# Four attention layers: the full layers start on their first twelve key tiles before the last keys exist

## The chip, the cores and the metric

The kernel runs on one core of one Trainium2 chip, in one launch. The metric is the device time of that launch in microseconds. Engines are named as the profile does: PE (TensorE matmul), PEld (its weight loads), DVE (VectorE), ACT (ScalarE), POOL (GpSimd) and SP (SyncE, whose queue issues the DMAs).

## The reference

Four layers of attention on 2048 tokens of width 512, 32 heads of 16. Layers 0 and 2 see a window of 256 keys, layers 1 and 3 ("full layers") all 2048.

```python
qkv = (x @ wqkv).reshape(B, S, 3, H, Dh).transpose(2, 0, 3, 1, 4)
scores = einsum("bhqd,bhkd->bhqk", q, k) * Dh ** -0.5      # window layers: masked to 0 <= i - j < 256
o = einsum("bhqk,bhkd->bhqd", softmax(scores), v)
x = x + o.transpose(0, 2, 1, 3).reshape(B, S, D) @ wo      # once per layer, on layernorm(x)
```

## The kernel before

**Tiles.** The tokens form four chunks of 512 (NQ), the heads eight quads of 4 (NQD) or four head groups of 8 (NHT). A full layer visits query chunks and quads (layer 1: chunk by chunk, all eight quads; layer 3: head group by head group, four chunks of two quads each). One visit (attn_full, line 805) walks 16 key tiles of 128 keys (NT). Each tile takes two score groups on PE (line 764), two exponentials on ACT (line 772) and, two score groups later, one P V group on PE (line 817), which sums into the pair of accumulators acc. After the 16th tile the epilogue (line 719) joins the two accumulators and normalises.

**The shift.** The exponential needs a bound on the scores. It comes from the largest squared key length of each head group: the key projection (keys, line 566) is followed by a product that sums squares (squares, line 548), a maximum on DVE (line 575), and, after the last chunk, key_shift (line 609), which writes the shift into row 7 of the keys in DRAM (kf). Only then may the keys of that head group be loaded into tiles kt (load_full, line 781).

**Side work.** Projections of other chunks and layers are Work objects: K1 and K3 (keys of the last chunk of layer 1, and of layer 3, by head group), Q, Q3 (queries), VV (values; half 0 are the first 16 heads), OO and O3 (output projection), T (transposes of the normalised rows by DMA). A Side (line 943) issues some of their matrix products after each tile. In a full layer each product is cut in 8 small matmuls, all products share one pair of PSUM banks (PH["halves"], lines 380 and 386), and each group of twelve is read out by two DVE steps (join, line 425) before the next may begin. Side.finish (line 1010) forces what is left of a list.

**The order.** The program writes PE's and DVE's instructions in the order in which they shall run in the full layers, by a clock that it keeps itself (clock, vt_). Between a window layer and the following full layer stands the tail (line 1231): the values of layer l + 1, the last output projection OO(l, 3) with the normalisation of the last chunk, its transposes, K1(0) and K1(1) or K3(3, 0), and two tiles of the last values (lasts, line 1233). The full layer starts when that is done. Its first keys and queries are loaded early (early_keys, early_queries, lines 629 to 637), and the shift of head group 0 is written into the loaded tile directly (line 622).

In layer 1 the list works[1][0] is spread over the first 64 tiles (quads 0 to 3 of chunk 0), works[1][1] over the rest. The keys of quads 2, 4 and 6 need the shifts of head groups 1, 2 and 3; a loop asks for them one quad ahead: 

```python
while (l, c, qd % 2) == (1, 0, 1) and qd + 1 in qds and ("S", 1, (qd + 1) // 2) not in DONE:
```

The generator wo (OO) ends its fourth step with the normalisation, in one of two places:

```python
            if i == 3 and not PH["full"]:
                if not tail:
                    yield "freed", clock[0]
                yield from norm(l + 1, c, xs, tail)
            yield last(MM)
        if PH["full"]:
            yield from norm(l + 1, c, xs, tail)
```

Of the kernel before, what the change touches and what calls it, by code (L numbers as in the profile page):

```python
# [19 lines left out]
P = 128  # L20
NT = S // P
# [169 lines left out]
def fast_path(ctx, tc, flag, a_x, a_wqkv, a_wo, b_wqkv, b_wo, out):  # L191
# [20 lines left out]
    XC, XN, V, O, OT, KM, PH = {}, {}, {}, {}, {}, {}, {"free": 0.0, "busy": False}  # L212
# [353 lines left out]
    def keys(l, c, act, ht=None, then=None, ring=0):  # L566
# [11 lines left out]
        pend.append((clock[0] + (4.6 if PH["full"] else 3.6 if PH["win"] else 1.2), rest))  # L578

    def queries(l, c, act, ht=None, ring=0):  # L580
# [23 lines left out]
        pend.append((clock[0] + (4.6 if PH["full"] else 3.6 if PH["win"] else 1.2), rest))  # L604
# [5 lines left out]
    def key_shift(l, ht):  # L610

        r = quarters(ht)
        kx = vp.tile([P, 1], F32, name=f"kx{l}_{ht}", tag="kx")
        nc.vector.tensor_reduce(kx[r], KM[l][r], axis=AX.X, op=ALU.max)
# [4 lines left out]
        nc.vector.tensor_scalar(m[r], ones[r], kx[r], -0.515, op0=ALU.mult, op1=ALU.mult)  # L619
        if ht == 0:  # L620
            for pr in range(2):
                nc.sync.dma_start(PRE["k"][7:P:R, pr, :].rearrange("r (c n) -> r c n", n=QC),
                                  m[2 * pr:2 * pr + 2, None, :].broadcast_to([2, 2, QC]))
        nc.sync.dma_start(rows(kf)[8 * ht:8 * ht + 8, 7, :].rearrange("h (c n) -> h c n", n=QC),
                          m[32 * ht:32 * ht + 8, None, :].broadcast_to([8, NQ, QC]))
        DONE["S", l, ht] = clock[0]

    PRE = {}

    def early_keys(l):  # L630

        PRE["k"] = pp.tile([P, 2, S // 2], F16, name=f"kt{l}_0_0_0", tag="kt", bufs=3)
        nc.sync.dma_start(PRE["k"], kf[0:2, :, :S // 2].rearrange("r p n -> p r n"))

    def early_queries(l):

        PRE["q"] = pp.tile([P, 2, QC], F16, name=f"qt{l}_0_0", tag="qt", bufs=3)
        nc.sync.dma_start(PRE["q"], qs[1, 0][0:2].rearrange("r p n -> p r n"))

# [78 lines left out]
    def epilogue(l, c, qd, a):  # L718
# [7 lines left out]
        with tc.high_priority(HEAD_START if l % 2 else 0):  # L726
            if l % 2:
                a = vp.tile([P, QC], F32, name=f"sa{n}", tag="j")
                join(a, acc, 1.0)
                vec(0.7)  # L730
# [21 lines left out]
        if u:  # L752
            soon(1, 1.2, parts)

# [26 lines left out]
    def load_full(l, c, qd):  # L781
        n = f"{l}_{c}_{qd}"
        pair = slice(2 * qd, 2 * qd + 2)
        qt, kts = PRE.pop("q", None), [PRE.pop("k")] if "k" in PRE else []
        if qt is None:
            qt = pp.tile([P, 2, QC], F16, name=f"qt{n}", tag="qt", bufs=3)
            nc.sync.dma_start(qt, qs[1, c][pair].rearrange("r p n -> p r n"))
        for v in range(len(kts), 2):
            kt = pp.tile([P, 2, S // 2], F16, name=f"kt{n}_{v}", tag="kt", bufs=3)
            nc.sync.dma_start(kt, kf[pair, :, v * S // 2:(v + 1) * S // 2].rearrange("r p n -> p r n"))  # L790
            kts.append(kt)
        return kts, qt

# [11 lines left out]
    def attn_full(l, c, qd, kt, qt, a):  # L805
        for j in range(NT):
# [6 lines left out]
            def pv(j=j, es_=es_):  # L813
                for h in range(4):
                    for r in range(2):
                        k = slice(R * r, R * r + R)
                        nc.tensor.matmul(acc[r][32 * h:32 * h + DH + 1, :], V[l, qd // 4, j // 8][k, j % 8, 4 * (qd % 4) + h, :],  # L817
                                         es_[h // 2][k, h % 2, :], start=(j == 0), stop=(j == NT - 1),
# [103 lines left out]
    class Side:  # L922
# [65 lines left out]
        def share(self):  # L988

            self.budget = min(self.budget + max((self.cost - self.spent) / max(self.steps - 3 - self.k, 1), self.least), 0.75)  # L990
            self.lag = max(self.lag - 0.42, -0.3)
# [5 lines left out]
            while (self.q and clock[0] >= PH["free"] and self.budget >= MM / 2 and (self.lag < 0.25 or self.budget > 0.45)  # L997
                   and self.spent - s0 < 1.5 * MM):
# [26 lines left out]
    def attention(l, works):  # L1025
# [3 lines left out]
        load = load_win if win else load_full  # L1029
        sd = None  # L1030
        for t in range(NHT if l == 3 else 1):
            for c in range(NQ):
                qds = range(2 * t, 2 * t + 2) if l == 3 else range(NQD)
                if l == 1:

                    sd = sd or Side(NT * NQD // 2, works[0], works[1], 0.33)
                    while ("Q", 1, c) not in DONE or pend and PH["busy"]:
                        sd.one(True)
                    settle()
                else:  # L1040
                    sd = Side((3 if win else NT) * len(qds), works[t * NQ + c], works[t * NQ + c + 1], 0.34 if l == 3 and t < 2 else 0.0)
                ahead = deque([PRE.pop("w", None) or load(l, c, qds[0])])
                if win:
                    ahead.append(load(l, c, 1))
                for qd in qds:
                    if (l, c, qd) == (1, 0, NQD // 2):
                        sd.finish()
                        sd = Side(NT * NQD * NQ - NT * NQD // 2, works[1], works[2], 0.33)
                    while (l, c, qd % 2) == (1, 0, 1) and qd + 1 in qds and ("S", 1, (qd + 1) // 2) not in DONE:
                        if ("K1", (qd + 1) // 2) in DONE and not PH["busy"]:  # L1050
                            settle()
                        else:
                            sd.one(True)
# [243 lines left out]
```

## Time and profile before

| | us |
|---|---|
| median of 3 runs | 2691.59 (2689.32 to 2695.28) |
| the profiled execution | 2692.26 |
| its span, first to last instruction | 2690.2 |
| PE busy, ACT busy, DVE busy | 2474.9, 2363.6, 1107.5 |
| mean granted clock of PE | 0.991 |

All times in the profile count from the start of the span. Matmuls are pipelined and their ends are modelled, so PE's cost is better read from the distance between starts than from busy time. The row of a group gives start, duration, engine, line, operation, tiles and shapes, and in brackets the idle time before it with what ended it.

### The profile page before, as it was taken

How to read it: one execution, taken by the hardware profiler on the slowest of the kernel's cores; microseconds unless marked ns; L12 is line 12 of the kernel's file. 1: busy time of each engine (PE TensorE's matmuls, PEld its weight loads, DVE VectorE, ACT ScalarE, POOL GpSimd, SP SyncE). 2: the span in 40 equal slices, each digit the busy share in tenths (PEclk: the TensorE clock that was granted, in tenths of full speed). 3: DMA queues.
4: the chain of work that ended last, by engine and by line, in shares of the span. 5: the costliest groups of instructions: out<-in, count | busy, mean ns of one | idle time of the engine just before them, and what ended most of it. 6: DMA issues, size and time to landing. Idle time of an engine off the chain costs nothing.

```text
span 2690.2 us, 120844 instructions
## 1 busy us (share of the span) xinstructions
PE 2474.9 (92%) x54767; PEld 1133.5 (42%) x54767; DVE 1107.5 (41%) x2350; ACT 2363.6 (88%) x2671; POOL 531.8 (20%) x1072
## 2 busy tenths in 40 slices
PE   7889999999998999999999999899999999999997
PEld 3344444444443444444444444544444443433332
DVE  5576453223334434434236666232333323333333
ACT  4666764999999999999996776699999999999997
POOL 1556550000000100100116886010000000000000
PEclk9999999999999999999999999999999999999999
DMA  8889875232334325324227666433333323334332
GB/s 281 254 274 268 236 198 155 69 97 86 110 94 120 97 91 148 103 87 115 92 77 211 189 171 166 128 95 105 98 97 97 106 77 114 106 98 126 126 118 93
DMA packets 341189, 361.29 MB, mean 134 GB/s; under 512 B 117800, under 2 KB 256568, under 8 KB 334392
## 3 DMA queue, kind: packets, MB, share of 16 engines
q1 hardware_dynamic: 340664, 353.46, 44.2%
q8 instruction: 430, 7.05, 1.1%
q14 instruction: 95, 0.78, 0.1%
HBM read 240.65 MB, written 96.99 MB: 126 GB/s over the span
## 4 chain that ended last, share of the span: by engine, by line
ACT 55%; PE 23%; issue 11%; DVE 6%; DMA 3%; SPq 1%; POOL 0%; ACTq 0%; DVEq 0%; POOLq 0%
ACT e L772 55%; PE b L406 7%; PE acc L850 4%; PE acc L817 3%; PE s L764 2%; PE s L768 2%; PE bs L409 2%; PE b L409 2%; PE b L402 1%; DMA kt<-kw 1%; DVE xh L461 1%; DVE xn L455 0%; DMA qs<-sp 0%; SPq L483 0%; DVE xh L455 0%
## 5 line engine op out<-in xcount | busy, mean ns | idle before, releaser
L772 ACT ACTIVATE e<-s 128x1024 f32<-128x1024 f32 (+2 forms) x2432 | 2241.6, 1056 | 143.2 <-PE s L768 104.5
L817 PE MATMUL acc<-e,vt 64*17 64x512 f32 x16384 | 1094.6, 590 | 1.9 <-issue 1.9
L764 PE MATMUL s<-qt,kt 64*32 64x512 f16 x16384 | 860.0, 381 | 123.9 <-ACT e L772 97.1
L764 PEld LDWEIGHTS <-kt 64*32 64x32 f16 x16384 | 408.2, 89 | 935.1 <-issue 853.8
L817 PEld LDWEIGHTS acc<-e,vt 64*17 64x17 f32 x16384 | 283.8, 92 | 67.9 <-issue 8.1
L843 POOL TENSOR_SCALAR_AFFINE_SELECT e<-e 128x256 f32<-128x256 f32 x512 | 230.5, 457 | 154.8 <-ACT e L772 154.1
L840 POOL TENSOR_SCALAR_AFFINE_SELECT e<-e 128x256 f32<-128x256 f32 x448 | 201.5, 456 | 96.5 <-ACT e L772 93.2
L850 PE MATMUL acc<-e,vt 128*17 128x384 f32 (+2 forms) x2816 | 202.6, 390 | 2.5 <-POOL e L840 2.2
L749 POOL TENSOR_TENSOR oh<-o,oh 128x512 f16<-128x512 f32 x31 | 36.1, 1165 | 725.1 <-DVE oh L748 725.1
L428 DVE TENSOR_SCALAR sa<-acc 128x512 f32<-128x512 f32 x64 | 44.3, 691 | 291.3 <-PE acc L817 291.3
L406 PE MATMUL b<-xc,w 128*32 128x512 f16 x2496 | 152.4, 389 | 10.8 <-DVE km L575 6.9
L714 DVE SCALAR_TENSOR_TENSOR x<-b,x 128x512 f32<-128x512 f32 x122 | 84.0, 689 | 175.1 <-PE b L402 168.4
L534 POOL TENSOR_TENSOR sq_h<-sp_h 128x512 bf16<-128x512 f16 x29 | 43.0, 1483 | 562.4 <-DVE sp_h L528 562.4
L768 PE MATMUL s<-qt,kt 64*128 64x384 f16 (+2 forms) x1408 | 120.8, 276 | 28.2 <-ACT e L772 22.7
L534 POOL TENSOR_TENSOR sq<-sp 128x512 bf16<-128x512 f16 x32 | 45.8, 1434 | 496.8 <-DVE sp L528 473.6
L402 PE MATMUL b<-xc,w 64*32 64x512 f16 x3072 | 126.4, 376 | 1.5 <-DVE j L429 0.8
L428 DVE TENSOR_SCALAR vt<-b 128x256 f32<-128x256 f32 (+1 forms) x36 | 18.4, 512 | 233.8 <-PE b L402 219.9
L402 PE MATMUL b<-wo,oh 64*32 64x512 f16 x2592 | 109.1, 376 | 4.1 <-DVE m_None L591 1.8
L402 PE MATMUL b<-xc,w_h 64*32 64x512 f16 x2784 | 111.8, 376 | 0.1
L428 DVE TENSOR_SCALAR j_h<-b 128x512 f32<-128x512 f32 x29 | 20.1, 692 | 214.6 <-PE b L402 214.6
L406 PEld LDWEIGHTS <-w 128*32 128x32 f16 x2496 | 73.5, 99 | 79.2 <-issue 27.7
L768 PEld LDWEIGHTS <-kt 64*128 64x128 f16 x1408 | 52.2, 94 | 125.7 <-issue 105.3
(142 smaller groups left out, 1942.3 us busy)
## 6 DMA issues: line engine op xcount, KB each, us to landing
kt<-kf SPq DMA_DIRECT2D x128, 512.0 KB
qt<-qs SPq DMA_DIRECT2D x128, 256.0 KB
xd<-x SPq DMA_DIRECT2D x96, 256.0 KB
x<-xd SPq DMA_DIRECT2D x96, 256.0 KB
w<-wd SPq DMA_DIRECT2D x21, 1024.0 KB
kt<-kw SPq DMA_DIRECT2D x64, 256.0 KB
qs<-sp SPq DMA_DIRECT2D x48, 256.0 KB
wo<-wd SPq DMA_DIRECT2D x12, 1024.0 KB
```

The costliest lines, as they stand in the source:

```text
L402: nc.tensor.matmul(ps[g:g + 32, r], a[k, g:g + 32], b[k], start=(i == 0), stop=(i == len(pairs) - 1), skip_group_check=True)
L406: nc.tensor.matmul(ps[g:g + 32], a[:, g:g + 32], b, start=(i == 0), stop=(i == len(pairs) - 1), skip_group_check=True)
L409: nc.tensor.matmul(ps, a, b, start=(i == 0), stop=(i == len(pairs) - 1))
L534: nc.gpsimd.tensor_tensor(sq, sp[:, 0], sp[:, 0], ALU.mult)
L714: nc.vector.scalar_tensor_tensor(xs[i], p, 1 / WS, xs[i], op0=ALU.mult, op1=ALU.add)
L764: nc.tensor.matmul(ps[g:g + 32, h], kt[R * h:R * h + R, pr, kc + g:kc + g + 32], qt[R * h:R * h + R, pr], start=True, stop=True, skip_grou ...
L768: nc.tensor.matmul(ps[:, h, s0:s0 + wd_], kt[R * h:R * h + R, pr, kc:kc + P], qt[R * h:R * h + R, pr, qc:qc + wd_], start=True, stop=True)
L772: nc.scalar.activation(e[:, :, w0:w1], ps[:, :, w0:w1], AF.Exp, scale=SCALE)
L817: nc.tensor.matmul(acc[r][32 * h:32 * h + DH + 1, :], V[l, qd // 4, j // 8][k, j % 8, 4 * (qd % 4) + h, :], es_[h // 2][k, h % 2, :], star ...
L840: nc.gpsimd.affine_select(v, v, pattern=[[0, 2], [-1, P]], compare_op=ALU.is_gt, fill=0.0, base=0, channel_multiplier=1)
L843: nc.gpsimd.affine_select(v, v, pattern=[[0, 2], [1, P]], compare_op=ALU.is_ge, fill=0.0, base=0, channel_multiplier=-1)
L850: nc.tensor.matmul(a[32 * h:32 * h + DH + 1, q * P:(q + nb) * P], V[l, (4 * c + j) // 4][:, j % 4, 4 * qd + h, :], es_[h // 2][:, h % 2, s ...
```

## The change

The full layers begin while the keys of the last chunk (512 keys, the last four tiles) do not exist yet.

- key_shift takes a number of chunks. first_loads calls it with three as soon as the window layer is done, and loads the queries, the first eight and the next four key tiles of quads 0 and 1.
- The visits of chunk 0, quads 0 and 1, are split: part A has tiles 0 to 11 of each, part B tiles 12 to 15 of each. After part A the sums are kept (park). When K1(0) or K3(3, 0) is done, key_shift writes the final shift, computes the ratio of the two exponentials into SH, and load_last fetches the last four tiles. The epilogue of part B multiplies the parked sums by the ratio and adds the new ones.
- Work leaves the tail for the side lists: T, K1(0) or K3(3, 0), the values of the last chunk; in layer 1 also K1(1) and the second half of values 1, in layer 3 also values of chunk 2. K1(3) goes from the first list of layer 1 to the second. OO(l, 3) is now of the kind without tail, and what is left of the tail when all its works are done or "freed" is carried into the full layer.
- In parts A and B ("rush") a tile may take 2.5 products of side work instead of 1.5, with a budget of 0.75 us.
- Keys of the next visit are loaded during a visit if they are complete, and otherwise when the visit begins, after its key projection and shift have been forced.

The core of the diff:

```diff
+    def first_loads(l):
+        key_shift(l, 0, NQ - 1)
+        HELD[0], HELD[1] = load_full(l, 0, 0), load_full(l, 0, 1)
+        load_more(l, 0, 0, HELD[0][0], True)
...
+    def park(l, c, qd):
+        drain(2)
+        a = PARK[c, qd] = vp.tile([P, QC], F32, name=f"pk{l}_{qd}", tag=("wa", "wc")[qd], bufs=1)
+        with tc.high_priority(HEAD_START):
+            join(a, acc, 1.0)
...
+    def load_last(l):
+        for qd in range(2):
+            nc.sync.dma_start(HELD[qd][0][1][:, :, S // 4:], kf[2 * qd:2 * qd + 2, :, 3 * S // 4:].rearrange("r p n -> p r n"))
...
+                if (c, qd) in PARK:
+                    nc.vector.scalar_tensor_tensor(a, PARK.pop((c, qd)), SH[l][:, 2 + qd:3 + qd], acc[0], op0=ALU.mult, op1=ALU.add)
+                    nc.vector.scalar_tensor_tensor(a, acc[1], 1.0, a, op0=ALU.mult, op1=ALU.add)
...
+        if not win:
+            visits[:2] = [(0, 0, qd, js) for js in (range(NT - 4), range(NT - 4, NT)) for qd in range(2)]
...
+            if (l, c, qd) == (1, 0, NQD // 2):
+                sd.finish()
+                sd = Side(NT * NQD * NQ - NT * NQD // 2, works[1], works[2], 0.33)
+            if not win and not part_a and (rest is None if part_b else not ahead):
+                while lacking(c, qd) or owing(c, qd):
+                    if lacking(c, qd) or PH["busy"]:
+                        sd.one(True)
+                    else:
+                        settle()
...
+                while part_a and u == 6 and ("V", l, 2, (0,), 0) not in DONE:
+                    sd.one(True)
+                while part_b and qd == 0 and u in (1, 3) and ("V", l, 3, (0,), u - 1) not in DONE:
+                    sd.one(True)
...
-    works = [[side0(c) for c in range(NQ)], [[last_lower(1), K1(2), upper(1, 2), upper(1, 3), K1(3)], side1()], [side2(c) for c in range(NQ)],
+    works = [[side0(c) for c in range(NQ)], [[T(1, 3), K1(0, True), VV(1, 3, False, (0,), (), range(2)), last_lower(1), K1(1, True), VV(1, 1, False, (1,)), K1(2, True), upper(1, 2), upper(1, 3)], side1()], [side2(c) for c in range(NQ)],
...
-    tails = {0: [VV(1, 2, True, (0,)), OO(0, 3, True), VV(1, 1, True, (0, 1), late(1)), VV(1, 0, True, (1,), late(1)), T(1, 3), K1(0, True), K1(1, True)],
-             2: [VV(3, 0, True, (0,)), OO(2, 3, True), VV(3, 1, True, (0,), late(3)), VV(3, 2, True, (0,), late(3)), VV(3, 0, True, (1,), late(3)), T(3, 3), K3(3, 0, True, True)]}
+    tails = {0: [VV(1, 1, True, (0,)), VV(1, 2, True, (0,)), OO(0, 3), VV(1, 0, True, (1,))],
+             2: [VV(3, 0, True, (0,)), VV(3, 1, True, (0,)), OO(2, 3)]}
```

What this does to the order of the instructions, at three places. First ACT where layer 1 begins (sp_1_3_h and sq_1_3_h are the products and squares of K1, vt the values, e the exponentials). Before:

```order
L519 ACTIVATE sp_1_3_h_0_7995<-bs_7982 128x512
L532 ACTIVATE sq_1_3_h_0_7998<-sp_1_3_h_0_7995 128x512
L519 ACTIVATE sp_1_3_h_1_8025<-b_8002 128x512
L532 ACTIVATE sq_1_3_h_1_8028<-sp_1_3_h_1_8025 128x512
L670 ACTIVATE vt_0_1_7684<-b_8034 128x16x16
L670 ACTIVATE vt_0_1_7684<-b_8056 128x16x16
L772 ACTIVATE e_0_0_0_0_8094<-s_0_0_0_0_8085 128x1024
```

And now:

```order
L672 ACTIVATE vt_1_0_7922<-bs_7924 128x16x16
L672 ACTIVATE vt_1_0_7922<-b_7938 128x16x16
L672 ACTIVATE vt_1_0_7922<-bs_7952 128x16x16
L672 ACTIVATE vt_1_0_7922<-b_7966 128x16x16
L786 ACTIVATE e_0_0_0_0_7996<-s_0_0_0_0_7987 128x1024
```

K1(0), K1(1) and the values of the last chunk no longer stand ahead of the first exponential.

Second, PE between quads 3 and 4 of layer 1, chunk 0 (s_0_3_15_1 is the last score group of quad 3, s_0_4_0_0 the first of quad 4). Before, 48 matmuls of K1(3) stand between them:

```order
L764 MATMUL s_0_3_15_1_11188<-qt_0_3_9609,kt_0_3_1_9613 32x512
L402 LDWEIGHTS w_1_3_h_10103
L402 MATMUL b_8076<-xc_3_7836,w_1_3_h_10103 32x512
...
L764 LDWEIGHTS kt_0_4_0_10433
L764 MATMUL s_0_4_0_0_11256<-qt_0_4_10431,kt_0_4_0_10433 32x512
```

Now there are 288 matmuls of the values of chunk 2, 384 of the values of chunk 3, together seven groups of 96 with a join after each, and the squares of K1(2):

```order
L778 MATMUL s_0_3_15_1_11183<-qt_0_3_9643,kt_0_3_1_10086 32x512
...
L402 MATMUL b_7986<-wv_2_1_0_9400,xc_2_7065 32x256
...
L402 MATMUL b_7986<-wv_3_1_0_10702,xc_3_8069 32x256
...
L556 MATMUL b_7986<-sq_1_3_h_2_10940,hsum 32x512
...
L778 MATMUL s_0_4_0_0_11894<-qt_0_4_11888,kt_0_4_0_11890 32x512
```

The same place on SP (mk_2 is the shift of head group 2, kt_0_4_0 the first keys of quad 4, kt_0_3 those of quad 3, w and wv weights). Before:

```order
L624 DMA kf<-mk_2_9250 8x4x512
L790 DMA kt_0_3_0_9611<-kf 128x2x1024
L787 DMA qt_0_4_10431<-qs_0_101 128x2x512
L373 DMA w_1_3_h_10103<-wd_1_110 128x8x128
L790 DMA kt_0_3_1_9613<-kf 128x2x1024
L790 DMA kt_0_4_0_10433<-kf 128x2x1024
```

And now:

```order
L798 DMA qt_0_6_12844<-qs_0_101 128x2x512
L371 DMA w_0_1_11954<-wd_0_109 128x4096
L371 DMA w_0_2_11956<-wd_0_109 128x4096
L620 DMA kf<-mk_2_11885 8x4x512
L808 DMA kt_0_4_0_11890<-kf 128x2x1024
```

The shift of quad 4 was stored before the keys of quad 3 were loaded; now it is stored right before quad 4's own keys.

Third, DVE early in layer 3, where the normalisation of chunk 3 ends (xn, xh its parts, mv the statistics, v, y, z the scaling). Before:

```order
L455 TENSOR_SCALAR xn_3_3_36886<-x_15_36718,mv_3_36796,y_3_36851 128x512
L461 TENSOR_TENSOR xh_3_3_36887<-xn_3_3_36886,xh_3_3_36887 128x512
L522 SCALAR_TENSOR_TENSOR sp_1_3_h_0_37085<-b_37072,sp_1_3_h_0_37085 128x512
L575 TENSOR_REDUCE km_34282<-b_37110 32x1
L614 TENSOR_REDUCE kx_0_37113<-km_34282 32x1
```

And now:

```order
L455 TENSOR_SCALAR xn_3_3_37869<-x_15_37536,mv_3_37610,y_3_37709 128x512
L455 TENSOR_SCALAR xh_3_3_37870<-x_15_37536,mv_3_37610,y_3_37709 128x512
L461 TENSOR_TENSOR xh_3_3_37870<-xn_3_3_37869,xh_3_3_37870 128x512
L46 TENSOR_SCALAR v_3_37930<-mv_3_37610 128x4
L47 TENSOR_SCALAR y_3_37931<-v_3_37930 128x4
...
L428 TENSOR_SCALAR vt_0_1_37874<-b_37670 128x16x16
```

After the last part the scaling starts again from the same statistics mv_3_37610, ahead of the first join of the values; the four parts follow a second time behind those joins. The generator wo was suspended inside the first normalisation when PH["full"] was switched on, and so meets both of its places.

More of the change, by code (lines that the diff above doesn't have):

```diff
@@ L803, in load_win, with attn_full @@
         return kt, qt
[L805 to L806 removed]
+    def attn_full(l, c, qd, kt, qt, js):
+        for j in js:
             es_ = []
@@ L1028, in attention @@
         phase(l)
[L1029 to L1033, printed above, removed]
-                if l == 1:
-                    sd = sd or Side(NT * NQD // 2, works[0], works[1], 0.33)
-                    while ("Q", 1, c) not in DONE or pend and PH["busy"]:
+        groups = [(c, range(2 * t, 2 * t + 2)) for t in range(NHT) for c in range(NQ)] if l == 3 else [(c, range(NQD)) for c in range(NQ)]
```

203 lines of the change are left out of this document (112 added, 91 removed).

## The prediction

> **What bounds the kernel now.** I read the chain of waits first, then busy time by stage, then the timelines at the two places where a window layer hands over to a full layer.
>
> ```profile
> ACT 55%; PE 23%; issue 11%; DVE 6%; DMA 3%; SPq 1%; POOL 0%; ACTq 0%; DVEq 0%; POOLq 0%
> ```
>
> More than half of the chain is ScalarE (ACT). By stage (length, then busy us of PE, PEld, DVE, ACT, POOL, granted clock, DMA share, GB/s):
>
> ```profile
> 400.00:450.00 50.00, 47.35 (x358) 26.21 (x351) 22.73 (x56) 16.21 (x33) 2.63 (x8) 1.00 0.63 180
> ...
> 1650.00:1700.00 50.00, 46.92 (x444) 28.34 (x437) 31.21 (x74) 20.06 (x32) 16.34 (x36) 1.00 0.81 206
> ...
> 2250.00:2300.00 50.00, 46.26 (x1138) 20.27 (x1123) 17.88 (x34) 50.00 (x56) 4.11 (x3) 1.00 0.36 103
> ```
>
> Inside a full layer ACT is busy 50.00 of 50; at the hand-overs it works 16 and 20 of 50 while PE is busy. In the chain in order of time, two starts one key tile apart:
>
> ```profile
> 465.71 0.87 ACT e L772
> ...
> 467.54 0.87 ACT e L772
> ```
>
> A tile costs ACT 1.83 us. So the time is this pace, times 512 tiles per full layer, plus every microsecond in which ACT has no exponential to do. PE's part of a tile:
>
> ```profile
> 2270.95 1.05 PE L817 MATMUL acc<-e,vt 64*17 64x512 f32 x16
> 2271.80 0.41 PE L764 MATMUL s<-qt,kt 64*32 64x512 f16 x8
> 2272.02 0.63 PE L402 MATMUL b<-xc,w_h 64*32 64x512 f16 x16
> ```
>
> From start to start a P V group takes 0.85 us and a score group 0.22, so a tile needs 0.85 + 2 x 0.22 = 1.29 us of PE and leaves 0.54 us for side work.
>
> **What the change wins.** PE at the hand-overs, and ACT's first exponential:
>
> ```profile
> 407.17 1.48 PE L409 MATMUL bs<-wv,xc 128*128 128x256 f16 x12
> ...
> 412.42 2.75 PE L409 MATMUL bs<-wo,oh 128*128 128x512 f16 x12
> ...
> 422.78 2.75 PE L409 MATMUL bs<-wv,xc 128*128 128x512 f16 x12
> ...
> 448.71 0.41 PE L764 MATMUL s<-qt,kt 64*32 64x512 f16 x8 [1.52 <-DMA kt<-mk]
> ...
> 1668.41 1.48 PE L409 MATMUL b<-wv,xc 128*128 128x256 f16 x12
> ...
> 1708.68 0.41 PE L764 MATMUL s<-qt,kt 64*32 64x512 f16 x8 [1.61 <-DMA kt<-mk]
> ```
>
> ```profile
> 449.26 4.69 ACT L772 ACTIVATE e<-s 128x1024 f32<-128x1024 f32 x5 [1.64 <-PE s L764]
> ```
>
> A V half (four groups) takes 412.42 - 407.17 = 5.25 us, the output projection 422.78 - 412.42 = 10.36. The new tail of layer 0 holds three V halves and the projection, 26.1 us: scores start at 433.3, not 448.71, 15.4 us earlier. The projection's weights now stand in SP's queue behind three key loads and wait for the buffer that the first V half frees; I charge 2 us (0 to 4). The tail of layer 2 holds two V halves and the projection, 20.9 us: scores start at 1689.3, not 1708.68, 19.4 us earlier. The waits for the shift in these rows went with a slower clock:
>
> ```profile
> 450.00:460.00 10.00, 9.02 (x208) 3.79 (x215) 0.00 (x0) 8.47 (x10) 0.00 (x0) 0.67 0.46 135
> ...
> 1710.00:1720.00 10.00, 8.63 (x216) 4.10 (x223) 0.00 (x0) 8.91 (x11) 0.00 (x0) 0.83 0.44 128
> ```
>
> ACT lost 1.5 and 1.1 us there; PE now crosses without a wait. **Won: 15.4 - 2 + 19.4 + 2.6 = 35.4 us** (31 to 38).
>
> **What it costs.** The tail's work did not vanish. It lies under the first tiles only where the order lets it, and at six places in the order PE has a block of side work, or a wait, between two score groups. When PE issues no scores for P us, two exponentials (1.83 us) are still under way, and the next starts 0.55 us after its scores (448.71 to 449.26), so ACT idles P + 0.55 - 1.83 = P - 1.3 us. Unit prices, first of a V group with no other work of PE in it (96 matmuls, then the two steps of its join on VectorE, DVE):
>
> ```profile
> 2192.86 1.51 PE L402 MATMUL b<-wv,xc 64*32 64x256 f16 x96
> ```
>
> ```profile
> 2194.44 0.42 DVE L428 TENSOR_SCALAR vt<-b 128x256 f32<-128x256 f32 x1 [3.54 <-PE b L402]
> 2194.90 0.42 DVE L429 SCALAR_TENSOR_TENSOR vt<-b,vt 128x256 f32<-128x256 f32 x1
> ```
>
> In a full layer all side products share one bank (line 386 of before), so the next group waits until 2194.90 + 0.42 = 2195.32: 2.5 us a group, about 1.3 of it PE. The chain behind the last product of a key projection (join, cast, square; then after the squares' product the maximum and the shift, and the store):
>
> ```profile
> 485.42 0.69 DVE L428 TENSOR_SCALAR j_h<-b 128x512 f32<-128x512 f32 x1
> ...
> 486.87 0.43 DVE L528 CAST sp_h<-j_h 128x512 f16<-128x512 f32 x1
> ...
> 496.53 1.22 DVE L575 TENSOR_REDUCE km<-b 32x1 f32<-32x1024 f32 x1 [2.46 <-PE b L556]
> ...
> 497.97 0.34 DVE L619 TENSOR_SCALAR mk<-ones,kx 32x512 f16<-32x512 f16 x1
> ```
>
> ```profile
> 487.44 1.48 POOL L534 TENSOR_TENSOR sq_h<-sp_h 128x512 bf16<-128x512 f16 x1 [81.16 <-DVE sp_h L528]
> ```
>
> ```profile
> L532 ACT ACTIVATE sq<-sp 128x512 bf16<-128x512 f16 x60 | 37.9, 631 | 4.4 <-PE b L559 3.4
> ```
>
> ```profile
> 446.90 1.77 DMA kt<-mk
> ```
>
> Join to square: 488.92 - 485.42 = 3.5 us with POOL's square, about 2.7 with ACT's (631 ns). The squares' product 0.4 (an estimate: a score group's 0.22 and a hand-over), maximum and shift 498.31 - 496.53 = 1.8, the store of the shift 1.8 (1.77 from issue to landing). Then the load of a half of the keys, 512 KB:
>
> ```profile
> 450.21 14.87 SPq L790 DMA_DIRECT2D kt<-kf  x3
> ```
>
> ```profile
> 467.00:468.00 1.00, 1.00 (x32) 0.43 (x26) 0.00 (x0) 1.00 (x2) 0.00 (x0) 1.00 0.74 279
> 468.00:469.00 1.00, 0.98 (x56) 0.63 (x48) 0.00 (x0) 1.00 (x2) 0.00 (x0) 1.00 0.06 16
> ```
>
> The third issue ends at 450.21 + 14.87 = 465.1 and its bytes end just after 468: 3.4 us with the issue itself; for 256 KB I estimate 2.4. The places, in order:
>
> - Layer 1, quad 1 to 2. The last 24 products of K1(1) and its squares stand right before the scores of quad 2, whose keys are loaded behind that shift; before, K1(1) was in the tail. P = 0.7 + 2.7 + 0.4 + 1.8 + 1.8 + 3.4 = 10.8; idle **9.5** (8 to 12).
> - Layer 1, quad 3 to 4. The first list is not done when its 64 steps are, and its rest is forced: seven V groups, then the squares of K1(2), the shift and the keys of quad 4, which wait for it; on SP the store stands behind two weight loads, one of which waits for the last V group. P = 7 x 2.5 + 0.4 + 1.8 + 1.8 + 3.4 = 24.9; idle **23.6** (16 to 28). Who waits: all scores of quad 4, so ACT.
> - Layer 3, tile 6 of quad 0. V of chunk 2 has left the tail and is forced here, 360 matmuls. DVE is late for its joins, because the normalisation of chunk 3 is queued twice, the second scaling ahead of them:
>
> ```profile
> 1685.89 0.17 DVE L46 TENSOR_SCALAR v<-mv 128x4 f32<-128x4 f32 x1
> ...
> 1688.35 0.54 DVE L455 TENSOR_SCALAR xn<-x,mv,y 128x512 f32<-128x512 f32 x1
> ...
> 1693.42 0.69 DVE L461 TENSOR_TENSOR xh<-xn,xh 128x512 f16<-128x512 f32 x1
> ```
>
>   One pass took 1694.1 - 1685.9 = 8.2 us; with the high half on DVE too I estimate 10. Starting 1.9 us after the projection's end (1689.3), it ends at 1701.3, the second scaling (2.5 us) at 1703.8; then one join and three groups to 1711. PE last issued scores 6.5 tiles after the start, at 1689.3 + 6.5 x 1.83 = 1701.2: P = 9.9, idle **8.6** (4 to 11).
> - Layer 3, end of part A. The second normalisation delays the transposes in the plan, so K3(3, 0) comes last: nine products (9 x 0.22 = 2.0), POOL's square, shift, and the last keys: 2.0 + 3.5 + 0.4 + 1.8 + 1.8 + 2.4 = 11.9; idle **10.6** (8 to 14).
> - Layer 3, part B: V of chunk 3 in two blocks of 3.2 and 3.7 us: idle **4.3**. At head group 1, two and a half V groups of 5.4 us: **4.1** (5 to 11 together).
> - The long waits should slow the clock as the two short ones did, 1.3 us each: **3.9** (0 to 10).
> - Three squares on ACT in layer 1 (1.9), two waits of ACT for DVE at the rescale's exponential (1.3), a lone V group (0.8), four more releases of the accumulator (2): **6** (2 to 12). The rescaling takes the place of a join's first step, and stands under tiles: nothing.
> - Costed at nothing: in layer 1 the squares of K1(0) stand 5.5 tiles (10 us) ahead of part B, and shift, store and last keys take 1.8 + 1.8 + 2.4 = 6.0 (if that cover is gone, 1 to 3 us). On SP the second keys of quad 1 now wait until tile 7 of quad 0 has freed a buffer; queued behind them are the stores of K1(0), whose products come two tiles later.
>
> In the row of 2250 to 2300 the clock is 1.00 with PE busy 46 of 50 us, so I keep a V group at 1.3 us of PE. The Trainium skill's page "TensorE: Matmul & The Clock Gate", section "A second HAM failure mode: psum-queue depth-cycling", speaks against this change: short pauses of PE between groups that cycle through PSUM can make the clock fall again and again. By it a V group would take 2.56 us of PE instead of 1.28, and the sum would be some 17 us higher; no run here shows it yet.
>
> **Sum:** 9.5 + 23.6 + 8.6 + 10.6 + 8.4 + 3.9 + 6 = 70.6 lost, 35.4 won: 35.2 us longer. The profiled run took 2692.26 us, 0.67 above the median of 2691.59: 2691.6 + 35 = **2727 us**.
>
> **The rivals.** (1) Faster. The blocks cost PE's time alone: joins, shifts and loads at the seams lie beside other tiles. Then the places cost 0, 8.1, 3.5, 1.1, 2.1, 1.9 and 6, together 22.7, and the time is 2679. It decides at the seam before quad 4: under 9 us of idle there and it holds. For it speaks that joins in the old layers lie beside tiles; against it, the order puts no tile between those groups. Chance 0.07. (2) No second delay in layer 3: DVE catches up, so its two first places cost 4.6 and not 19.2: 2712. Chance 0.14, inside the range. (3) The clock falls in the V blocks as it fell in the two slices above (about 13 groups at half clock, 1.28 us more each): 2727 + 17 = 2744, with longer waits behind them up to 2760. Chance 0.12. (4) The early start fails: shift and loads come late in the tail, and half of the 35 us is not won: 2744. Chance 0.04. (5) Gain and losses within 0.2%: 2686 to 2697. Chance 0.03.
>
> **How the numbers follow.** The forecast has the remaining 0.60, with 2700 (low ends of the losses) to 2754 (high ends). A measurement of this kernel can tell about 0.2%, 5 us, from no change. Faster 0.07, same 0.03, slower 0.90. Range 2700 to 2754: it holds the forecast's bounds, (2), (4) and half of (3).
>
> **What would show it.** Right: first exponentials of the full layers at about 436 and 1715 (1690 plus the 25 us that layer 1 nets by the list: 40 lost, 15 won); ACT gaps of 8 to 12 us before quad 2 and over 16 before quad 4 of layer 1; two of about 9 and 11 us early in layer 3, the second released by a load of keys; 50.00 of 50 elsewhere. Wrong: no gap over 5 us at those seams, V groups that follow each other faster than 2.4 us, or scores of quads 2 and 4 that wait for no DMA.

## The result and the profile after

The changed kernel takes 2756.56 us (median of 4 runs, 2756.11 to 2760.64), the kernel before 2690.45 beside it: a ratio of 1.024 with a 95% interval of 1.0226 to 1.0254. It is slower, as forecast, but by 65 us in the profiled spans (2755.1 against 2690.2) and not by 35, and 2.6 us beyond the upper end of the range.

The shares of the chain of waits, to be held against the 55, 23 and 11% of before:

```profile
ACT 52%; PE 26%; issue 11%; DVE 7%; DMA 3%; POOL 1%; SPq 1%; ACTq 0%; DVEq 0%
```

PE has taken from ACT. Where, a table shows that follows ACT's exponentials through the two profiled executions (layer = first to last exponential of it, hand-over = last of one to first of the next):

| us | before | after | difference |
|---|---|---|---|
| start and layer 0 | 404.1 | 402.9 | -1.2 |
| hand-over to layer 1 | 45.2 | 32.5 | -12.7 |
| layer 1 | 952.6 | 1001.4 | +48.8 |
| hand-over to and layer 2 | 259.7 | 260.0 | +0.3 |
| hand-over to layer 3 | 47.7 | 27.5 | -20.2 |
| layer 3 | 959.9 | 1000.5 | +40.6 |
| last exponential to the end | 21.0 | 30.3 | +9.3 |

The early start is there, and the two hand-overs are 12.7 and 20.2 us shorter. ACT's first exponentials of layers 1 and 3, and then each row of ACT's timeline with a long wait ahead of it:

```profile
435.34 4.69 ACT L786 ACTIVATE e<-s 128x1024 f32<-128x1024 f32 x5
...
509.94 1.02 ACT L786 ACTIVATE e<-s 128x1024 f32<-128x1024 f32 x1 [9.60 <-PE s L778]
...
600.76 1.02 ACT L786 ACTIVATE e<-s 128x1024 f32<-128x1024 f32 x1 [28.69 <-PE s L778]
...
1724.30 12.94 ACT L786 ACTIVATE e<-s 128x1024 f32<-128x1024 f32 x14 [10.41 <-PE s L778]
1745.28 8.55 ACT L786 ACTIVATE e<-s 128x1024 f32<-128x1024 f32 x9 [8.04 <-PE s L778]
...
1789.62 1.02 ACT L786 ACTIVATE e<-s 128x1024 f32<-128x1024 f32 x1 [5.02 <-PE s L778]
...
1807.68 1.02 ACT L786 ACTIVATE e<-s 128x1024 f32<-128x1024 f32 x1 [5.36 <-PE s L778]
...
2002.95 1.02 ACT L786 ACTIVATE e<-s 128x1024 f32<-128x1024 f32 x1 [6.69 <-PE s L778]
```

Layer 1 starts at 435.34 (436 was forecast), layer 3 at 1724.30 (1715 was forecast; layer 1 lost 9 us more than the forecast's 40 by then). The waits stand at the forecast places: ahead of quads 2 and 4 of layer 1, at tile 6 and at the end of part A of layer 3, in part B, and at head group 1. Below, a gap is the distance between the starts of two exponentials less the 0.92 us of one; a small instruction of ACT inside it does not shorten it.

The longest, in the chain of waits (start, length, what):

```profile
575.99 1.55 PE b L402 x96
577.53 0.02 issue
577.56 0.44 DVE vt L428
578.00 0.02 issue
578.02 0.44 DVE vt L429
...
582.51 1.63 issue
584.14 0.44 PE b L402 x14
...
585.54 2.81 PE b L402 x70
...
591.81 0.40 PE b L556 x2
592.22 0.02 issue
592.24 1.23 DVE km L575
...
594.05 1.81 DMA kf<-mk
595.90 0.03 issue
595.93 4.03 DMA kt<-kf
```

This is the forecast chain: value (V) groups 2.51 us apart (575.99 to 578.50), the squares, the maximum, the store of 1.81, and a load of keys of 4.03 where 3.4 was taken. Two things were not forecast: a halt (PE stands still) of 1.63 inside a group in which PE waits for nothing that the profile names, and the group behind it that takes 2.81 where the others take 1.5.

The granted clock (column 8) at the first long wait:

```profile
500.00:505.00 5.00, 0.61 (x2) 0.10 (x1) 2.10 (x4) 0.34 (x1) 0.00 (x0) 0.52 0.28 85
505.00:510.00 5.00, 0.82 (x16) 0.35 (x24) 0.00 (x0) 0.06 (x1) 0.00 (x0) 0.50 0.81 267
510.00:515.00 5.00, 4.88 (x104) 1.72 (x89) 1.14 (x2) 2.83 (x3) 0.00 (x0) 0.62 0.14 51
```

The clock fell behind PE's wait for the squares of K1(1), 2.64 us ahead of 500.39, and PE comes out of the wait for the keys at half clock. The next two exponentials follow after 2.13 and 2.08 us, not 0.92; below, these are slow steps.

The end, which the prediction did not look at; PE's timeline behind the last scores:

```profile
2724.23 0.41 PE L778 MATMUL s<-qt,kt 64*32 64x512 f16 x8
2724.44 0.84 PE L402 MATMUL b<-wo,oh 64*32 64x512 f16 x24
2726.82 0.84 PE L402 MATMUL b<-wo,oh 64*32 64x512 f16 x24 [1.54 <-DVE x L716]
2729.20 1.48 PE L402 MATMUL b<-wo,oh 64*32 64x512 f16 x24 [1.54 <-DVE x L716]
2732.22 1.48 PE L402 MATMUL b<-wo,oh 64*32 64x512 f16 x24 [1.54 <-DVE x L716]
2733.45 3.12 PE L839 MATMUL acc<-e,vt 64*17 64x512 f32 x32
```

The whole output projection of chunk 2 (96 matmuls) stands behind the last scores and ahead of the last values: 2733.45 - 2724.44 = 9.0 us. Before, it was done two tiles ahead of the end; the lists of layer 3 had taken in values of chunks 2 and 3, and what was last in them fell off (the run with 2.0 products below).

### The profile page after: what moved, and what is told of

Read it like the earlier page. It is cut to its first block, busy times and chain, and to the rows that moved or that the text cites. A ratio compares the mean times of both kernels' runs of the same rounds, so it can differ in the third digit from the quotient of the medians.

```text
span 2755.1 us, 124191 instructions
## 1 busy us (share of the span) xinstructions
PE 2485.0 (90%) x56414; PEld 1145.7 (42%) x56414; DVE 1145.3 (42%) x2437; ACT 2354.6 (85%) x2647; POOL 528.2 (19%) x1071
## 4 chain that ended last, share of the span: by engine, by line
ACT 52%; PE 26%; issue 11%; DVE 7%; DMA 3%; POOL 1%; SPq 1%; ACTq 0%; DVEq 0%
ACT e L786 51%; PE b L406 8%; PE acc L839 4%; PE acc L872 4%; PE b L402 3%; PE s L778 3%; PE s L782 2%; PE bs L409 1%; PE b L409 1%; DMA x<-in_A_x_dram 1%; POOL e L865 1%; POOL e L862 1%; DVE xh L461 1%; DVE x L716 0%; DVE xn L455 0%
## 5 line engine op out<-in xcount | busy, mean ns | idle before, releaser
L402 PE MATMUL b<-wv,xc 64*32 64x256 f16 (+1 forms) x4992 | 119.0, 297 | 17.0 <-DVE vt L429 13.1
L402 PE MATMUL b<-xc,w_h 64*32 64x512 f16 x3072 | 120.6, 376 | 0.0
L428 DVE TENSOR_SCALAR vt<-b 128x256 f32<-128x256 f32 (+1 forms) x52 | 25.3, 486 | 228.2 <-PE b L402 228.2
L402 PE MATMUL b<-wo,oh 64*32 64x512 f16 x2592 | 109.2, 381 | 10.6 <-DVE x L716 9.1
```

Source lines behind the costliest of these rows:

```text
L402: nc.tensor.matmul(ps[g:g + 32, r], a[k, g:g + 32], b[k], start=(i == 0), stop=(i == len(pairs) - 1), skip_group_check=True)
L428: nc.vector.tensor_scalar(dst, ps[0], scale, None, op0=ALU.mult)
```

## The experiments

All ratios are to the kernel before, measured beside each run (2691 to 2692 us). Executions of one kernel spread over 4 to 18 us, in stages that no edit touched as well (start and layer 0 took 402.2 to 409.5 us in the profiles here), so each verdict rests on the gap at the place first and on the total second.

**One normalisation.** The generator remembers that it has normalised:

```diff
             if i == 3 and not PH["full"]:
...
+                early = True
                 yield from norm(l + 1, c, xs, tail)
...
-        if PH["full"]:
+        if not early:
             yield from norm(l + 1, c, xs, tail)
```

> The normalisation of chunk 3 runs once in layer 3, all else as in the changed kernel. Theory (the loss is the sum of the places where the order puts side work or a key chain between two score groups): the transposes come earlier, both blocks of the values of chunk 3 leave part B and one group of them joins the block ahead of it. The gap at tile 6 stays at 8 us, the gap at the end of part A is 11 to 14 us (12.2 now), the two gaps in part B (2.8 and 5.5, with 2 us of slow tiles behind them) go: 9 us less, about 2747 us. Rival (PE has too much side work early in layer 3, so idle time that goes in one place comes back in another): 2753 to 2758. The prediction's own account of the gap at tile 6, that DVE is late there because of the second normalisation, would take 4 us or more from that gap.

Measured: 2751.0 us, ratio 1.0221 (1.0195 to 1.0246). The two gaps in part B are gone (2.8 and 5.5 us); the gap at the end of part A grew from 12.2 to 15.6, since a V group joined the block there. At tile 6:

```profile
1745.12 1.02 ACT L787 ACTIVATE e<-s 128x1024 f32<-128x1024 f32 x1 [9.23 <-PE s L779]
```

That gap did not shrink (8.2 in the changed kernel, 9.4 now). So the prediction's account of it, DVE late by the second normalisation, falls. The changed kernel's own trace shows it too; PE in the forced block there:

```profile
1738.08 1.50 PE L402 MATMUL b<-wv,xc 64*32 64x256 f16 x96 [1.08 <-DVE vt L429]
1740.59 1.50 PE L402 MATMUL b<-wv,xc 64*32 64x256 f16 x96 [1.00 <-DVE vt L429]
```

The joins are as quick as anywhere, and the four V groups alone make the gap. Nor does the gap at the end of part A need the second normalisation. Layer 3 became 4.6 us shorter (1000.5 to 995.9) and not 9: part of the idle time moved on to the next place. The median fell by 5.6 us, but in that profile layer 1, which the edit does not touch, is 5.4 shorter as well.

**2.0 products per tile in layer 3.**

```diff
-                   and self.spent - s0 < (2.5 if rush else 1.5) * MM):
+                   and self.spent - s0 < (2.5 if rush else 2.0 if PH["three"] else 1.5) * MM):
...
+        PH["three"] = l == 3
```

> In layer 3 alone a tile may take 2.0 products of side work instead of 1.5, so that a V group takes four tiles and not five. In the order the 96 matmuls of the output projection of chunk 2 that stood behind the last scores stand under them again, and the block at head group 1 shrinks from 240 to 160 matmuls. Theory: the time from the last exponential to the end falls from 30.3 us to the 21 of the kernel before, and the gap at head group 1 by about 2: 2745 us. Rival (the 9 us at the end are the slow clock and the epilogue, and the bigger pieces push scores back in every tile that has one): 2754 to 2760.

Measured: 2746.8 us, ratio 1.0194 (1.0164 to 1.0224). From the last exponential to the end 20.8 us; PE's timeline there:

```profile
2724.68 0.41 PE L778 MATMUL s<-qt,kt 64*32 64x512 f16 x8
2724.89 2.52 PE L839 MATMUL acc<-e,vt 64*17 64x512 f32 x32
```

The projection is under the tiles again; the gap at head group 1 fell from 6.9 to 2.6. The missing 9.3 us are these 96 matmuls, as the theory had it. Layer 3 itself fell by 4.1 us (1000.5 to 996.4), where the smaller gap and the slow step behind it make 5.4, so its other tiles gave back some 1.3 us.

**PE kept busy in the wait.** Ahead of quads 2 and 4 of layer 1:

```diff
+            if (l, c) == (1, 0) and qd in (2, 4):
+                for _ in range(30):
+                    nc.tensor.matmul(PH["halves"][:, 0], XC[1, 3][:, 0, 0, :P], XC[1, 3][:, 0, 0, :], start=True, stop=True)
             ops = HELD[qd] if part_a or part_b else ahead.popleft()
```

> PE gets 30 matmuls of 128x128x512 without use (6.4 us at full clock) right ahead of the first scores of quads 2 and 4 of layer 1, so that it is busy while it would wait for the keys. Theory (after such a wait the granted clock is half, and the next tiles take 2.13 us per exponential instead of 0.91 for that reason): the clock stays at 1.00 there, the two slow steps behind each wait go, 2.4 us each, and the time is 2751 to 2753 us. Rival (the slow steps are the refill of the pipeline of scores, exponentials and values, not the clock): 2756 to 2758.

Measured: 2751.8 us, ratio 1.0227 (1.0202 to 1.0251). ACT behind the two waits:

```profile
516.32 2.10 ACT L786 ACTIVATE e<-s 128x1024 f32<-128x1024 f32 x2 [11.51 <-PE s L778]
...
606.17 4.09 ACT L786 ACTIVATE e<-s 128x1024 f32<-128x1024 f32 x4 [29.78 <-PE s L778]
```

Both slow steps are gone (two exponentials in 2.10, four in 4.09), so it is the clock and not the refill of the pipeline. But the matmuls themselves held the scores back, by 1.9 us ahead of quad 2, where PE had already waited 2.64 us for the squares and the first of them ran at half clock, and by 1.1 ahead of quad 4. Net at the two places: 1.8 us won of 4.8. The rest of the 4.7 us in the total is not explained by the edit, so that the total lies where it was expected is luck.

**K1(2) first.**

```diff
-... K1(1, True), VV(1, 1, False, (1,)), K1(2, True), upper(1, 2), upper(1, 3)] ...
+... K1(1, True), K1(2, True), VV(1, 1, False, (1,)), upper(1, 2), upper(1, 3)] ...
```

> K1(2) goes ahead of the second half of values 1 in the first list of layer 1; the number of products is the same. Ahead of quad 4 now stand 720 matmuls of values (seven and a half groups) and no squares; shift and keys of quad 4 come under tiles of quad 3. Theory (place by place): the gap ahead of quad 4 falls from 28.9 us to 7.5 x 2.5 + 0 to 3 - 1.3 = 18 to 20.5 us, without a wait for keys and with at most one slow step: 2745 to 2748 us. Rival (the list as a whole is too long, and what leaves this gap comes back in quads 2 and 3): 2754 to 2758.

Measured: 2744.7 us, ratio 1.02 (1.0168 to 1.0232); the gap ahead of quad 4 fell from 28.9 to 22.2 us, with one slow step left. PE inside it:

```profile
587.93 1.28 PE L402 MATMUL b<-wv,xc 64*32 64x256 f16 x80 [1.01 <-DVE vt L429]
590.92 0.41 PE L402 MATMUL b<-wv,xc 64*32 64x256 f16 x16 [1.70 <-issue]
592.34 2.37 PE L402 MATMUL b<-wv,xc 64*32 64x256 f16 x96 [1.00 <-DVE vt L429]
595.68 2.76 PE L402 MATMUL b<-wv,xc 64*32 64x256 f16 x96 [0.98 <-DVE vt L429]
```

No wait for keys is left. The chain of squares, shift and keys took 8.2 us in the changed kernel (591.81 to 600.00), where 7.4 were charged. The gap is over its 18 to 20.5 us by the halt and two groups at half clock.

**Weight loads later.** On that kernel, the two loads of 1 MB that SP issues in the gap are held until quad 4 runs:

```diff
+        if n in ("1_0_1", "1_0_2"):
+            nc.scalar.activation(w[0:1, 0, 0, 0:1], PH["e"][0:1, 0, 0:1], AF.Copy)
         if f1 - f0 == D:
             nc.sync.dma_start(w, wd[ty, s])
...
+            if PH.get("hold"):
+                return
...
+                PH["hold"] = True
                 sd.finish()
...
+                if (l, c, qd, u) == (1, 0, NQD // 2, 3):
+                    PH["hold"] = False
```

The copy writes into the weights' buffer and reads the newest exponentials, so the load waits for them; "hold" keeps other works from opening meanwhile.

> As the kernel with K1(2) ahead (2744.7 us, a gap of 22.2 us ahead of quad 4, in which PE stood still for 1.7 us inside a V group and the groups after it took 2.4 and 2.8 us), but the two weight loads of 1 MB that SP issued in that gap wait until the second tile of quad 4 has been exponentiated. Theory (PE runs out of instructions there because the fetch of its next 16 KB stands behind those loads, and the halt then lowers the clock): no halt over 0.5 us in the seven groups, every group about 1.5 us, the gap 17.5 to 19 us, 3 to 5 us less in all: 2740 to 2742 us. Rival (matmuls that follow each other this fast outrun the fetch by themselves): halt and gap stay, 2744 to 2746 us.

Measured: 2745.2 us, ratio 1.0194 (1.017 to 1.0218). PE's two halts in the block, and ACT behind it:

```profile
584.00 0.85 PE L404 MATMUL b<-wv,xc 64*32 64x256 f16 x48 [0.48 <-issue]
...
587.74 0.41 PE L404 MATMUL b<-wv,xc 64*32 64x256 f16 x16 [0.61 <-issue]
```

```profile
593.51 2.10 ACT L788 ACTIVATE e<-s 128x1024 f32<-128x1024 f32 x2 [18.89 <-PE s L780]
```

The halt of 1.70 became two of 0.48 and 0.61, no group ran at half clock, the gap fell from 22.2 to 19.1 and the slow step went. This speaks for the theory and does not prove it. It is one profile against one; without the edit the same block had halts of 1.63 in the changed kernel, 0.81 in the run with one normalisation, and 0.98 and 2.06 in the one with PE kept busy. And the two halts that are left came with the DMA engines at 0.00 to 0.07, so the loads do not make all of it. The total missed its 2740 to 2742 and lies in the rival's range (2745.2 against 2744.7), and layer 1 as a whole took 989.0 us against 989.4: what the gap gained was lost elsewhere in the layer.

**K1(1) first**, right behind K1(0):

```diff
-... K1(0, True), VV(1, 3, False, (0,), (), range(2)), last_lower(1), K1(1, True), ...
+... K1(0, True), K1(1, True), VV(1, 3, False, (0,), (), range(2)), last_lower(1), ...
```

> K1(1) goes right behind K1(0) in the first list of layer 1, all else as in the changed kernel. In the order the squares of K1(1) stand four tiles ahead of quad 2; two V groups (192 matmuls) come together in part B ahead of quad 1, and ahead of quad 4 stand 576 matmuls of values and no squares. Theory (place by place): the gap ahead of quad 2 falls from 11.8 us to 0 to 2; a new gap of 4 to 6 us in part B; the gap ahead of quad 4 falls from 28.9 us to 6 x 2.5 + 0 to 3 - 1.3 = 14 to 17 us; with the slow steps that go: about 2732 us (2728 to 2737). Rival (too much side work in the list, the idle time only moves): over 2745 us.

Measured: 2734.1 us, ratio 1.0157 (1.013 to 1.0183): 22 us from the order of one list. No gap is left ahead of quad 2; 4.6 us in part B; ahead of quad 4

```profile
587.80 1.03 ACT L786 ACTIVATE e<-s 128x1024 f32<-128x1024 f32 x1 [18.10 <-PE s L778]
```

18.2 us where 14 to 17 were expected, with no wait for keys: a halt of 1.13 and three groups at half clock behind it stand in the block.

**All together.** These edits in one kernel (2.0 products in all layers), and in layer 1 the last half of values 3 in the second list, asked for ahead of tile 12 of quad 4; the first half of values 2 of layer 3 either in the tail or first in layer 3's list.

> All the edits together: the normalisation once, 2.0 products a tile, K1(1) right behind K1(0), the last half of values 3 of layer 1 in the second list and only asked for ahead of tile 12 of quad 4, and the first half of values 2 of layer 3 back in the tail. Theory (place by place): layer 1 loses 8 to 12 us at its seams instead of 45, layer 3 10 to 14 instead of 42, its start is 5.2 us later, the end 9 us shorter: 2688 us (2680 to 2700), about the kernel before. Rival (idle time moves): over 2715 us.

> As the one with all the edits, but the first half of values 2 of layer 3 is not in the tail and stands first in layer 3's list: 208 of its matmuls are forced at tile 6. Theory: layer 3 starts 5.2 us earlier and loses about 4 us at tile 6, so the time is within 3 us of the other's: 2687 us (2680 to 2700). Rival (V groups cost the same wherever they stand): 5 us less than the other.

Measured: 2707.4 us (ratio 1.006, 1.0038 to 1.0081) and 2706.8 (1.0056, 1.0032 to 1.008): some 50 us of the 65 are back, but not the 69 that the places add up to: both times lie above the expected 2680 to 2700, though within 3 us of each other, as was expected. In part the rest stands where the losses were (7.8 us at the end of part A of layer 3 in the first), in part at places that were no places before; ACT ahead of quad 6 of layer 1 in the first of them:

```profile
634.60 1.02 ACT L787 ACTIVATE e<-s 128x1024 f32<-128x1024 f32 x1 [4.96 <-PE s L779]
```

K1(3) and, ahead of chunk 1, Q(1, 1) now come late in the second list: 5.1 and 4.9 us and their slow steps. So idle time does move in part, to the chain that is next in the list.

**Mended.** In layer 2's tail the projection goes ahead of the last value halves, and the second list of layer 1 begins with the values, K1(3) and Q(1, 1) at a budget of 0.45. Three forms: half of values 2 in the tail, all of it (shown here), and the first with the early projection in the tail of layer 0 too.

```diff
-             2: [VV(3, 0, True, (0,)), VV(3, 1, True, (0,)), VV(3, 2, True, (0,)), OO(2, 3)]}
+             2: [VV(3, 0, True, (0,)), OO(2, 3), VV(3, 1, True, (0,)), VV(3, 2, True, (0,))]}
...
+        a = [K1(3, True), Q(1, 1, False)] + a + [*[OO(1, c) for c in range(3)], Q(1, 2, False), Q(1, 3, False)]
```

> All the edits of the version with the tail (2707 us), and three more: in the tail of layer 2 the output projection goes ahead of the last value halves, so that the normalisation of chunk 3 lies beside them; half of values 2 of layer 3 in the tail, half first in the list; the second list of layer 1 begins with the last half of values 3, K1(3) and Q(1, 1) at a budget of 0.45. In the order the squares of K3(3, 0) stand five tiles ahead of part B and those of K1(3) four tiles ahead of quad 6, and the queries of chunk 1 are done six tiles ahead of it. Theory (the change pays when no key chain and no block of values stands between two score groups): the gaps before quad 6 and chunk 1 (5.1 and 4.9 us and their slow steps) and before part B of layer 3 (7.8 us) go: 2680 us (2674 to 2688), 10 us faster than the kernel before. Rival (what is cleared in one place comes back in another, as it did in part in the version with the tail): 2692 to 2707 us.

> As the mended one, but all of the first half of values 2 of layer 3 in the tail: layer 3 starts 2.6 us later, and one V group of two leaves the block in part B. Theory: 2682 us, within 3 us of the mended one. Rival as there: 2692 to 2707 us.

> As the mended one, but in the tail of layer 0 too the output projection goes second. K1(0) and K1(1) then start four tiles earlier in the order. Theory: one V block less in part B of layer 1, 1 us, against a wait for the projection's weights in the tail of 3 to 5 us more: 2681 to 2684 us.

Measured: 2705.9 us (ratio 1.0056, 1.0041 to 1.007), 2698.4 (1.0032, 1.0021 to 1.0043) and 2696.5 (1.0021, 1.0008 to 1.0034). All three missed, the first two by coming out in the rival's range. The gaps that they were made for are gone; a new one of 9.9 to 10.2 us stands ahead of chunk 1 of layer 3 in all. In the second form, PE:

```profile
1758.81 0.46 PE L556 MATMUL b<-sq_h,hsum 64*32 64x512 bf16 x2 [3.62 <-POOL sq_h L534]
1764.77 0.63 PE L779 MATMUL s<-qt,kt 64*32 64x512 f16 x8 [5.50 <-DMA qt<-qs]
```

K3(3, 0) had moved ahead of Q3(1, 0), and the query chain had become the one without cover: 9.9 us. The wait for the weights expected of the third form did not come: its hand-over to layer 1 is 3.0 us shorter (29.8 against 32.8), since PE's wait of 2.77 for these weights in the other forms is gone. The first form is 7 us slower than the second. In the profiles its layer 3 is 9.4 longer (985.4 against 976.0), and 4 us of that are a gap, in which PE waits 2.82 for weights of the values, and a slow step behind it; the rest was not followed up.

**Queries first.** The second form with the early projection in layer 0's tail and Q3(1, 0) first in layer 3's list:

```diff
-        a += [Q3(c + 1, t)] if c < 3 else []
+        a = ([Q3(c + 1, t)] + a if (t, c) == (0, 0) else a + [Q3(c + 1, t)]) if c < 3 else a
```

> As the mended one with all of values 2 in the tail (2698 us), with the early output projection in the tail of layer 0 as well, and with Q3(1, 0) first in layer 3's list: its squares then stand 23 tiles ahead of chunk 1, those of K3(3, 0) four tiles ahead of part B. Theory (every key or query chain that stands at a seam costs its whole length there, and nothing where tiles cover it): the gap of 10 us ahead of chunk 1 of layer 3, which came with the mended order, goes with its slow steps, and no gap over 3 us takes its place: 2684 to 2690 us, level with the kernel before or up to 6 us faster. Rival (idle time moves on to the next seam): 2694 to 2700 us.

Measured: 2684.0 us (5 runs, 2678.22 to 2685.61), ratio to the kernel before 0.9961 (0.9947 to 0.9974): 7 us faster than the kernel before and 73 faster than the change as it was made, as expected. ACT where layer 3 begins:

```profile
1699.73 38.18 ACT L787 ACTIVATE e<-s 128x1024 f32<-128x1024 f32 x41
1738.00 0.20 ACT L630 ACTIVATE sh<-sh 32x1 f32<-32x1 f32 x1
1738.11 6.48 ACT L787 ACTIVATE e<-s 128x1024 f32<-128x1024 f32 x7
```

The first 48 exponentials (part A and the exponential of the ratio) run without a wait; before the change the same stretch had its clock and load waits, after it the gap of 8.2, and that of 12.2 at its end.

Not all is covered. In layer 1 a gap of 3.9 us and a slow step of 2.0 stand in part B, where the earlier forms had 3.1 to 4.6, and a gap of 2.7 behind a halt of 2.77 in quad 4. The hand-overs are 15.4 and 13.9 us shorter than before the change, but layer 1 is still 16.2 us longer (968.8) and layer 3 4.7 (964.6).

## Why the prediction was right in kind and short in size

The sign, the six places and the win were right. The sum was 70.6 lost and 35.4 won. By the two profiles it was as follows (won is 34.1 from the first table and 2.2 of clock behind the hand-overs; "small" is what remains):

| term | predicted | measured |
|---|---|---|
| won: hand-overs, clock behind them | 35.4 | 36.3 |
| layer 1, quad 1 to 2 | 9.5 | 11.8 |
| layer 1, quad 3 to 4 | 23.6 | 28.9 |
| layer 3, tile 6 | 8.6 | 8.2 |
| layer 3, end of part A | 10.6 | 12.2 |
| layer 3, part B | 4.3 | 8.3 |
| layer 3, head group 1 | 4.1 | 6.9 |
| slow steps behind the long waits | 3.9 | 10.9 |
| small | 6 | 4.7 |
| the end | none | 9.3 |
| lost | 70.6 | 101.2 |

**The step that failed** is the sum of the losses, 30.6 us too low. It has no term for the end: the prediction followed the work that left the tail to the seams where the order forces it, and not to the end of layer 3, where lists that had grown pushed out the last projection. The run with 2.0 products brought the projection back under the tiles, and with it the 9.3 us. **The second mis-sized term** is the clock: 3.9 was taken from before's two short waits at 1.3 each, but at five places the long waits and halts cost 1.6 to 2.4, 10.9 in all, and the run with PE kept busy showed that it is the clock. **The third** are halts inside V blocks, 1.63, 2.2 and 1.31 us at the seam before quad 4, in part B and at head group 1, and a group at half clock behind the first: together 6.4 of the 12.1 us that these three places have over their forecasts (the cause of the other 5.7 stays open). The forecast took a V group at 2.5 us, and without a halt it is 2.51. The loads of keys at the two seams of layer 1 took 4.5 (504.67 to 509.18) and 4.03 us, not 3.4.

**The step on tile 6** had the right number for a wrong reason, so that 8.2 came out for 8.6 is luck: DVE was not late, the four groups are enough. The clock that the win was to bring back came back in full only in layer 3. In layer 1 PE crossed with no wait over 0.99, and the granted clock still fell to 0.87 and 0.79 in the rows of 435 to 440 and 440 to 445.

**The rivals.** (1) Blocks cost PE's time alone: no, the joins stand in the chain. (2) No second delay in layer 3: its premise held at tile 6, where DVE kept up, but not its price; the gaps were 8.2 and 12.2 us. (3) The clock falls in V blocks: not by the joins. Four groups with waits of 1.00 between them kept 1.50 to 1.64 each; it fell behind the halts, and in the projections at the end, where waits of 1.54 made the third group take 1.48 where the first took 0.84. The rule quoted from the Trainium skill's page "TensorE: Matmul & The Clock Gate", section "A second HAM failure mode: psum-queue depth-cycling", agrees with the end, where pauses of 1.54 us stand between groups of 0.84, and not with these joins, where pauses of 1.00 stand between groups of 1.50. (4) and (5) did not occur.

**The idea itself** is not refuted: with most of the chains covered, the kernel is 0.4% faster than the one before, and what the change lost, it lost by the order of its lists. That the 0.4% is the early start's alone is not shown, since the kernel before was not run with 2.0 products and the larger budget.

## What to carry to other kernels

When work leaves a serial stretch for the shade of another engine, follow it to all the places where it can come out again: the seams where something asks for it, and the end of the last list. A chain of projection, squares, shift, store and load costs its whole length (8 to 12 us here) where it stands at a seam and nothing four tiles earlier, so within a list the chains go first and the products that nothing reads soon go last; and when one chain has been covered, look which one is next, since here each mended seam laid bare another. A sum over places was too low here as long as such chains were left in the lists.

## What the runs showed of the hardware

**PE can stand still for its instructions in dense runs of small matmuls.** This is read from the records. Each halt of PE over 1.2 us in a V block of the changed kernel begins with no releaser in the profile and ends 1.3 to 1.5 us after a 16 KB block of the instruction queue has landed (in the trace's DMA records, 581.83 to 582.81 ahead of PE's 584.14; 1804.91 to 1805.84 ahead of 1807.13; 1999.35 to 2000.34 ahead of 2001.81). In the slice of a microsecond in which each of these fetches begins, or in the one ahead of it, the DMA engines (column 9) were busy at 0.90 or more:

```profile
580.00:581.00 1.00, 0.14 (x13) 0.00 (x0) 0.77 (x2) 0.00 (x0) 0.00 (x0) 1.00 0.98 418
...
1804.00:1805.00 1.00, 0.92 (x72) 0.64 (x48) 0.01 (x1) 0.00 (x0) 0.00 (x0) 1.00 1.04 381
...
1998.00:1999.00 1.00, 0.21 (x16) 0.00 (x0) 0.69 (x2) 0.00 (x0) 0.00 (x0) 1.00 0.90 289
```

The other profiles agree. From 430 us on, all fourteen together have 29 such halts over 1.2 us, in V blocks and elsewhere, and each ends 1.2 to 1.6 us after such a block has landed. None follows a fetch with the DMA engines under 0.2 busy in the microsecond ahead of it (2809 fetches); with 0.9 and more, 17 of 897 were followed by one. So busy DMA engines go with these halts, but most fetches behind them cost nothing. Moving two loads of 1 MB took one halt from 1.70 to 0.48 and 0.61 us, with the reservations above; for the other two places of the changed kernel this was only read from the records. The Trainium skill's page "Runtime: NRT & Kernel Launch", section "Instruction fetch mechanics", has the fetch mostly hidden; in these blocks it was not.

**Pauses and the clock.** The length of one pause does not tell here whether the clock falls. Four waits of 1.00 us in a row left it at 1.00, and so did a single one of 2.49 in the tail of layer 0 of the changed kernel:

```profile
419.10 2.76 PE L409 MATMUL bs<-wo,oh 128*128 128x512 f16 x12 [2.49 <-DMA wo<-wd]
```

Yet behind the halts of 1.63 and 2.21 us groups took twice the time or nearly so, and behind one of 0.81 in the run with one normalisation a group took 2.81 and not 1.50. In between it went either way: behind a halt of 1.31 us at head group 1 the scores took 0.81 and not 0.41, behind one of 1.35 in layer 1 the clock stayed at 1.00. Thirty matmuls without use, put into waits of 8.18 and 7.80 us, had the clock back at 1.00 by the time the scores came, but cost most of what they saved, because they ended after the awaited keys had landed.
